# A new load order on two queues, a bf16 product for u, and half of the stores on GpSimd's queue, in an attention and MoE kernel on one core

## The chip, the cores and the metric

The kernel runs on one core of a Trainium2 chip. The metric is the time of one execution on the device in us; lower is better. A profile is one execution with the hardware profiler; its span, from the first instruction to the last, is some 2 us shorter than the time. A run over 1.5% above the fastest of its kernel is called slow, the others fast. Ratios and profiles are of fast runs unless a sentence says otherwise; medians are of all runs, slow ones too (one of the changed kernel's four in the result, three of a_dummy's six). PE is TensorE, PEld its weight loads, ACT ScalarE, DVE VectorE, POOL GpSimd, SP SyncE; a "q" behind a name is that engine's sequencer, which issues transfers. A transfer has landed when its data are there and its semaphore, a counter that others wait for, says so.

## The reference

Inputs r, k, v, w are 4 x 8 x 768 x 48 (batch, heads, tokens, width) in fp32, u is 8 x 48, w_in 384 x 1024, w_out 1024 x 384. The output is 3072 x 384, fp32.

```python
# attention, for each token t
cur = einsum('bhd,bhe->bhde', u * k[t], v[t])
y[t] = einsum('bhd,bhde->bhe', r[t], state + cur)
state = w[t][..., None] * state + einsum('bhd,bhe->bhde', k[t], v[t])
# x: y as 3072 tokens x 384, then
h = x @ w_in
solu = h * softmax(h)
ln = (solu - mean(solu)) / sqrt(var(solu) + 1e-6) * g_ln
out = ln @ w_out
```

## The kernel before

The 3072 tokens are 24 units of 128 (chunk c of batch b). A unit needs four loads of 192 KB (w, k, r, v). What each engine does, and in which order, is written in one string, ORDER. Each word is a stage, a unit number and, after the point, who does it or which PSUM bank it uses: `LW5.s` loads w of unit 5 from SP's queue, `LV4.a` loads v of unit 4 from ScalarE's. Every engine keeps to the written order, so **a transfer that cannot be issued holds up everything that is written behind it on the same engine**.

```python
ORDER = """
... kr2.d y0.a p3 M1.b0 LK5.a S1.s2 dg2 krk3.s3 vb2.a m1.d krr3 et1 wi0.a S2.s0 wi1.p M2.b1 st1 X0.s1 kr3.a m2.d
Y1.is2 LR4.s wi2.p et2 y1.a M3.b0 xT0.d LV4.a X1.s3 q3 m3.d H0.b1 dv2 gw1.a dg3 gw2.d e0 Y2.is2 LW5.s xT1.d
gw3.p st2 H1.b0 y2.a he0 lw4 gw0.a X2.s1 LR5.s e1 gw7.d cum4.b1 gw4.d hot2.s3 gw6.d gw5.d ex4 he1 vb3.p mn0.s3
LW6.s LV5.a dv3 xT2.a LK6.s kp4 S3.s0 mc0 Y3.is2 LR6.s lw5 ce6.d krk4.s1 ce3.d hq0.a cum5.b0 ce4.d krr4 ce2.d
H2.b1 ce7.d ex5 LW7.s ce1.d ce5.d ce0.d y3.a LK7.s p4 kp5 et3 Oa0.s3 ...            # cut: the other lines
"""
NIO = 7                                   # input buffers of each kind

queue = {"s": sp, "a": act}

def load_w(i, x):                         # LW; LK, LR, LV are alike
    queue[x].dma_start(out=w_t[i % NIO][:, :, :D], in_=rows_of(w, i))

def load_w_in(j, x):                      # LI: a third of w_in, 512 KB
    queue[x].dma_start(out=win_f[:, j, :], in_=moe_w_in[j * 128:(j + 1) * 128, :])

def load_w_out(j, x):                     # LO: a half of w_out, 768 KB
    part = slice(j * KF // 2, (j + 1) * KF // 2)
    queue[x].dma_start(out=wout_f[:, part, :],
                 in_=moe_w_out.rearrange("(ko ki) d -> ki ko d", ki=128)[:, part, :])

def spread_u(i, x):                       # us
    ps["u"] = bank([C, DM], F32, x, "u_ps")
    pe.matmul(ps["u"], lhsT=ones_row, rhs=u_row, start=True, stop=True)

def cast_w_in(j, x): ...                  # wi: a third of w_in to bf16
def gain(f, x): ...                       # gw: an eighth of w_out times g_ln, to bf16
def column_mean(i, x): ...                # mn, mc: mean of w_out's columns, on TensorE
def centre(f, x):                         # ce: an eighth of w_out less that mean
    (dve if x == "d" else pool).tensor_add(out=w2[:, f, :DM], in0=w2[:, f, :DM], in1=mean_sb)

def warm_up(i, x): ...                    # hot: i products that nobody reads

def store(i, x):                          # out
    c, b = units[i]
    sp.dma_start(out=out[b * S + c * C:b * S + (c + 1) * C, :], in_=o_t[i % NWK])
# ... cut: a unit's stages: lw, cum, ex, kp, krk/krr (transposes), M (scores), Y (attention), S (state),
#     X (x transposed), H (hidden, needs all of w_in), e and he and hq (exp, product, square),
#     Oa/Ob (output product, needs all eighths of w_out centred), sq/qm/lv/o (variance and scale)
```

The softmax here doesn't subtract the row's maximum and nothing guards it: scores larger than these inputs give would overflow.

Of the kernel before, what the change touches and what calls it, by code (L numbers as in the profile page):

```python
# [555 lines left out]
```

## Time and profile before

| | before |
|---|---|
| time, median of 3 runs | 154.34 us (153.63 to 155.8) |
| span of the profiled run, granted clock | 151.6 us, 0.994 |
| busy share PE / DVE / ACT / POOL | 91 / 84 / 78 / 63% |
| first exp of the hidden layer (e0) starts | 24.51 us |
| cumulative sum of unit 5 starts | 31.63 us |
| mean of w_out's columns copied | 31.16 us |
| first output product starts | 33.73 us |
| last output product ends | 147.2 us |

The prediction below shows the lines for the first reading. One row and one group are added here, because the changed kernel answers to them: the clock granted to TensorE in 40 slices (tenths), and VectorE's timeline (start, busy time, engine, line, operation, tiles, count, idle time before it).

```profile
PEclk9999999999999999999999999999999999999997
...
31.19 2.48 DVE L89 TENSOR_TENSOR w<-w,mean_sb 128x384 bf16<-128x384 bf16 x8 [0.35 <-ACT mean_sb L89]
```

The row tells of no throttling up to the end, but its first record is of 13 us. Before that TensorE was slower: one cumulative product takes 0.50 us at 12.81 us and 0.33 from 14 us on. The eight subtractions of the mean, the last thing that the first output product waits for, take 0.31 us each.

### The profile page before, as it was taken

Reading aid. Unit: us, or ns where it says so; the run is one execution under the profiler, and the core shown is the slowest. Engines: PE = TensorE matmul, PEld = TensorE weight load, DVE = VectorE, ACT = ScalarE, POOL = GpSimd, SP = SyncE. Lnnn points to the kernel's source line nnn. Section 1 sums busy time; section 2 is a strip of 40 time slices with the busy share of each in tenths; the row PEclk is TensorE's granted clock in tenths of the full one; section 3 lists DMA queues with packets and bytes.
Section 4 is the critical chain, followed back from the end, with each engine's and each line's share of the span. In section 5 each row is a group of like instructions: output and inputs, shape, how many; then the busy total and the mean of one; then the engine's idle time right before and its main releaser. Section 6 shows DMA issues by size and latency. Waiting matters only on the chain.

```text
span 151.6 us, 5258 instructions
## 1 busy us (share of the span) xinstructions
PE 137.2 (91%) x2156; PEld 106.6 (70%) x2158; DVE 127.9 (84%) x235; ACT 117.9 (78%) x238; POOL 94.9 (63%) x127
## 2 busy tenths in 40 slices
PE   4799787879999997999988999999999999999980
PEld 1145566467788776888777797878887888889650
DVE  5209797999999996999976999999998998688940
ACT  3465766599999997999798688999898997484442
POOL 7484993531879859993849999299847682500000
PEclk9999999999999999999999999999999999999997
DMA  5999999999983999989699999898950111011142
GB/s 110 259 257 334 405 335 255 178 210 188 224 179 121 229 217 193 215 176 241 142 243 208 230 175 232 162 230 193 248 164 6 52 56 52 4 52 56 52 160 104
DMA packets 104825, 27.08 MB, mean 179 GB/s; under 512 B 100313, under 2 KB 104418, under 8 KB 104802
## 3 DMA queue, kind: packets, MB, share of 16 engines
q1 hardware_dynamic: 94256, 24.26, 69.6%
q10 hardware_dynamic: 10546, 2.49, 7.3%
q8 instruction: 17, 0.28, 0.7%
q14 instruction: 6, 0.05, 0.1%
HBM read 22.03 MB, written 4.72 MB: 176 GB/s over the span
## 4 chain that ended last, share of the span: by engine, by line
PE 54%; DMA 12%; SPq 10%; DVE 8%; ACT 6%; POOL 4%; issue 4%; ACTq 0%; POOLq 0%
PE o_ps L89 22%; PE h_ps L89 13%; SPq L89 10%; DMA w_in<-in_w_dram 6%; PE kr_ps L89 4%; PE y_ps L89 4%; DMA kr_in<-in_r_dram 4%; PE s_ps L89 3%; PE cum_ps L89 3%; PE m_ps L89 3%; DMA v_in<-in_v_dram 3%; PE x_ps L89 2%; DVE he L89 1%; POOL m L89 1%; DVE w L89 1%
## 5 line engine op out<-in xcount | busy, mean ns | idle before, releaser
L89 PE MATMUL o_ps<-w,he 128*128 128x385 bf16 x192 | 45.7, 325 | 0.1
L89 PE MATMUL h_ps<-xT,win_sb 128*128 128x128 bf16 x576 | 35.9, 219 | 0.3 <-DVE xT L89 0.3
L89 PEld LDWEIGHTS <-win_sb 128*128 128x128 bf16 x576 | 33.0, 98 | 0.9 <-issue 0.4
L89 PE MATMUL o_ps<-inv_col,e 128*128 128x1 bf16 x192 | 31.7, 165 | 0.0
L89 DVE TENSOR_TENSOR he<-h_ps,e 128x1024 bf16<-128x1024 f32 x24 | 29.1, 1216 | 2.7 <-ACT e L89 2.5
L89 PE MATMUL o_ps<-one_col,hq 128*128 128x1 bf16 x192 | 31.3, 163 | 0.0
L89 ACT ACTIVATE e<-h_ps 128x1024 bf16<-128x1024 f32 x24 | 24.5, 1020 | 4.7 <-PE h_ps L89 4.6
L89 DVE TENSOR_TENSOR kp<-cum_ps,kr_in 128x768 bf16<-128x768 f32 x24 | 22.7, 948 | 5.9 <-ACT cum_ps L89 5.6
L89 PEld LDWEIGHTS <-hq 128*128 128x128 bf16 x192 | 18.5, 96 | 12.8
L89 POOL TENSOR_TENSOR p<-kr_in 128x384 bf16<-128x384 f32 x24 | 24.4, 1018 | 3.7 <-DMA kr_in<-in_r_dram 3.6
L89 POOL TENSOR_TENSOR dv<-vb,dg 128x384 bf16<-128x384 bf16 x24 | 19.8, 830 | 9.6 <-DVE dg L89 7.4
L89 POOL TENSOR_SCALAR_AFFINE_SELECT m<-m 128x1024 bf16<-128x1024 bf16 x15 | 16.8, 1120 | 13.4 <-ACT sq L89 5.8
L89 POOL TENSOR_TENSOR q<-p,u_bc 128x384 bf16<-128x384 bf16 x24 | 21.8, 911 | 1.9 <-ACT u_bc L89 1.7
L89 PEld LDWEIGHTS <-kp 128*128 128x128 bf16 x272 | 17.4, 98 | 6.0 <-DVE kp L89 2.1
L89 ACT ACTIVATE cum_ps<-cum_ps 128x768 f32<-128x768 f32 x24 | 19.2, 802 | 3.0 <-PE cum_ps L89 2.9
L89 PE MATMUL kr_ps<-ident,kp 128*128 128x128 bf16 x192 | 18.0, 222 | 2.3 <-ACT gr L89 0.8
L89 PEld LDWEIGHTS <-he 128*128 128x128 bf16 x192 | 18.4, 96 | 0.9
L89 PEld LDWEIGHTS <-e 128*128 128x128 bf16 x192 | 18.4, 96 | 0.5 <-issue 0.2
L89 ACT ACTIVATE lw<-w_in 128x384 bf16<-128x384 f32 x24 | 12.4, 523 | 4.1 <-DMA w_in<-in_w_dram 4.1
L89 ACT CAST m<-m_ps 128x1024 bf16<-128x1024 f32 x15 | 15.0, 1013 | 0.7 <-PE m_ps L89 0.6
L89 DVE TENSOR_TENSOR m<-m_ps,keep 128x1024 bf16<-128x1024 f32 x9 | 10.9, 1215 | 4.2 <-PE m_ps L89 4.2
L89 ACT ACTIVATE hq<-he 128x1024 bf16<-128x1024 bf16 x13 | 13.7, 1057 | 0.0
(82 smaller groups left out, 262.5 us busy)
## 6 DMA issues: line engine op xcount, KB each, us to landing
kr_in<-in_r_dram SPq DMA_DIRECT2D x24, 192.0 KB, 4.3
out_dram<-o SPq DMA_DIRECT2D x24, 192.0 KB, 3.2
kr_in<-in_k_dram SPq DMA_DIRECT2D x21, 192.0 KB, 3.5
w_in<-in_w_dram SPq DMA_DIRECT2D x21, 192.0 KB, 4.2
v_in<-in_v_dram SPq DMA_DIRECT2D x20, 192.0 KB, 4.1
...
```

The source lines that it names most:

```text
L89: made = make(*args, **kwargs)
```

## The change

It is meant to get the inputs in earlier by giving ScalarE's queue 17 of the front's loads in place of 12, in a new order, to make u's product one pass, and to free SP of the later stores. Three of the eight subtractions of the mean go from VectorE to GpSimd.

```diff
 ORDER: first line and what matters of the front (all of the string is new)
-LW0.a LK0.s LU0.a LR0.s LW1.a LW2.s hot4.s3 LG0.s LK1.s lw0 LV0.a ...
+LW0.a LW1.s LU0.a LR0.s LK0.a LR2.s hot5.s3 LK1.a LW2.s LR1.a lw0 LG0.a LV0.s ur0 lw1 us0.s0 LW3.a ...
+et0 m1.d LV3.a q2 LI0.s gc0 lw4 LI1.a kp2 cum3.b0 LW5.s Y0.ns3 st0 ex3 cum4.b1 krk2.s1 y0.d vb1.a LO1.s kp3
+X0.s2 LI2.a krr2 dv1 LK5.s ex4 xT0.d krk3.s0 dg2 p3 Y1.ns3 LW6.s S1.s2 kr2.a kp4 p4 LO0.a M2.b0 krr3 et1 m2.d
+vb2.a krk4.s1 q3 kr3.a krr4 dv2 y1.d vb3.a M3.b1 dg3 LV4.a Y2.is0 wi1.p st1 S2.s3 LR5.a kr4.d wi0.a m3.d M4.b0
+wi2.p X1.s2 S3.s1 y2.a et2 LV5.a X2.s0 m4.d dv3 H0.b1 gw1.a xT1.d gw0.d H1.b0 et3 gw3.d e0 LK6.s q4 st2 st3 lw5
 ... cut; the centring: ce4.d ce3.d ce1.d ce0.d ce6.p ce7.d ce2.p ce5.p; the stores: out0 to out11, out12.p to out23.p
-ones_row = consts.tile([1, C], F32)
+ones_row = consts.tile([1, C], BF16)
+u_b = consts.tile([1, DM], BF16)
-queue = {"s": sp, "a": act}
+queue = {"s": sp, "a": act, "p": pool}
+def round_u(i, x):                        # ur
+    dve.tensor_copy(out=u_b, in_=u_row)
-    pe.matmul(ps["u"], lhsT=ones_row, rhs=u_row, start=True, stop=True)
+    pe.matmul(ps["u"], lhsT=ones_row, rhs=u_b, start=True, stop=True)
-    sp.dma_start(out=out[...], in_=o_t[i % NWK])
+    queue[x or "s"].dma_start(out=out[...], in_=o_t[i % NWK])
```

More of the change, by code (lines that the diff above doesn't have):

```diff
@@ L21 @@
 ORDER = """
-LW0.a LK0.s LU0.a LR0.s LW1.a LW2.s hot4.s3 LG0.s LK1.s lw0 LV0.a cum0.b0 LR1.s us0.s0 ex0 hot2.s3 uc0 lw1 LV1.s
-p0 kp0 LW3.a LK2.a LR2.s krk0.s3 q0 krr0 cum1.b1 kr0.a hot2.s2 LV2.s LK3.a M0.b0 LR3.s p1 gs0.s1 ex1 m0.d
-hot3.s3 LI1.s lw2 q1 dg0 cum2.b0 lw3 hot2.s3 kp1 vb0.p LI0.a S0.s2 dv0 vb1.a dg1 hot1.s3 ex2 Y0.is0 et0 LV3.a
-cum3.b1 LI2.s p2 kp2 krk1.s3 gc0 LO0.s ex3 st0 LW4.s krk2.s1 q2 krr1 LO1.s krr2 kp3 kr1.a hot3.s2 dv1 LK4.s
-kr2.d y0.a p3 M1.b0 LK5.a S1.s2 dg2 krk3.s3 vb2.a m1.d krr3 et1 wi0.a S2.s0 wi1.p M2.b1 st1 X0.s1 kr3.a m2.d
@@ L27 @@
-Y1.is2 LR4.s wi2.p et2 y1.a M3.b0 xT0.d LV4.a X1.s3 q3 m3.d H0.b1 dv2 gw1.a dg3 gw2.d e0 Y2.is2 LW5.s xT1.d
-gw3.p st2 H1.b0 y2.a he0 lw4 gw0.a X2.s1 LR5.s e1 gw7.d cum4.b1 gw4.d hot2.s3 gw6.d gw5.d ex4 he1 vb3.p mn0.s3
-LW6.s LV5.a dv3 xT2.a LK6.s kp4 S3.s0 mc0 Y3.is2 LR6.s lw5 ce6.d krk4.s1 ce3.d hq0.a cum5.b0 ce4.d krr4 ce2.d
-H2.b1 ce7.d ex5 LW7.s ce1.d ce5.d ce0.d y3.a LK7.s p4 kp5 et3 Oa0.s3 lw6 e2 LR7.s kr4.d p5 krk5.s2 cum6.b0 st3
-hq1.a Ob0 vb4.p he2 LW8.s q4 krr5 ex6 S4.s1 LK8.s kr5.d sq0 M4.b1 lw7 Oa1.s0 kp6 et4 m4.a LR8.s X3.s2 qm0 st4
@@ L32 @@
-vb5.p M5.b0 xT3.a cum7.b1 dg4 sel4 lv0 krk6.s1 LV6.s Ob1 m5.d ex7 LW9.s dv4 lw8 S5.s2 kp7 o0.a krr6 LK9.s p6
-cum8.b0 sq1 et5 Y4.ns3 kr6.d ex8 H3.b1 q5 LV7.s y4.d hq2.a kp8 q6 LR9.s krk7.s1 e3 X4.s3 st5 LW10.s vb6.p M6.b0
-krr7 xT4.d Oa2.s2 dg5 m6.a LK10.s qm1 kr7.d dv5 krk8.s3 lv1 Ob2 he3 out0 sel6 o1.a lw9 M7.b0 out1 dg6 S6.s1 sq2
-m7.a LV8.s hq3.d krr8 cum9.b1 LR10.s Y5.ns0 vb7.p qm2 kr8.d lv2 H4.b0 p7 LW11.s et6 y5.d ex9 st6 p8 lw10 kp9
-LV9.s X5.s3 S7.s0 e4 Oa3.s1 q7 o2.d vb8.a he4 out2 cum10.b1 dv6 xT5.a krk9.s2 et7 LK11.s ex10 Y6.ns3 q8 krr9 st7
@@ L37 @@
-LV10.s H5.b0 hq4.a kp10 sel7 LR11.s kr9.a y6.d M8.b1 dg7 LW12.s S8.s0 lw11 m8.d Ob3 dv7 et8 e5 LV11.s vb9.p
-krk10.s3 st8 X6.s2 LK12.s p9 M9.b1 he5 xT6.a Y7.ns0 sq3 m9.a krr10 LR12.s S9.s2 dg8 cum11.b0 et9 LW13.s y7.d
-H6.b1 lw12 dv8 ex11 kr10.d LK13.s p10 qm3 lv3 kp11 Oa4.s0 LR13.s e6 q9 st9 X7.s3 cum12.b0 LW14.s xT7.a Ob4 he6
-p11 ex12 LV12.s krk11.s2 sel9 sq4 Y8.ns3 o3.a kp12 H7.b1 hq5.a out3 vb10.p qm4 y8.d q10 LK14.s lv4 dg9 M10.b0 e7
-Oa5.s1 LR14.s m10.d vb11.p q11 o4.a krr11 LW15.s X8.s3 lw13 dg10 Ob5 p12 xT8.a out4 he7 kr11.a S10.s0 dv9 S11.s3
@@ L42 @@
-LV13.s dg11 sq5 hq6.a Y9.ns2 vb12.p qm5 cum13.b0 y9.d dv10 LK15.s H8.b1 et10 ex13 st10 LR15.s et11 lw14 kp13
-Oa6.s2 LW16.s e8 hq7.d krk12.s0 lw15 M11.b0 p13 st11 LK16.s Ob6 lv5 he8 o5.a q12 krr12 m11.a Y10.ns3 out5 kr12.d
-krk13.s1 cum14.b1 LR16.s y10.d sq6 krr13 sel11 ex14 cum15.b0 LW17.s kr13.d Oa7.s0 ex15 qm6 LV14.s kp14 p14
-Y11.ns3 lw16 X9.s1 Ob7 kp15 lv6 dv11 LK17.s vb13.a xT9.d p15 o6.a M12.b1 y11.d M13.b0 m12.a X10.s1 out6 m13.d
-krk14.s2 q13 S12.s3 LR17.s hq8.a krr14 H9.b1 dg12 LV15.s vb14.p xT10.d sq7 q14 et12 qm7 st12 LW18.s lv7 krk15.s1
@@ L47 @@
-dg13 e9 X11.s3 sel12 H10.b0 o7.d kr14.a out7 he9 dv12 LK18.s Y12.ns0 xT11.a p16 krr15 LR18.s Oa8.s2 e10 y12.d
-kr15.d q15 LV16.s cum16.b1 he10 S13.s0 ex16 dv13 Ob8 LV17.s et13 kp16 q16 X12.s3 LW19.s Y13.ns1 sq8 xT12.a st13
-M14.b0 vb15.p M15.b1 LK19.s m14.a y13.d krk16.s3 S14.s0 hq9.d krr16 LR19.s m15.a S15.s1 p17 qm8 kr16.d H11.b0
-LW20.s et14 dg14 lv8 sel14 st14 et15 LK20.s dg15 H12.b1 e11 vb16.p o8.d sel15 st15 out8 lw17 Oa9.s3 he11 LV18.s
-e12 vb17.p dv14 S16.s0 LV19.s hq10.a he12 Ob9 dv15 LR20.s et16 cum17.b0 st16 q17 Y14.ns2 LV20.s ex17 X13.s1
@@ L52 @@
-y14.d M16.b1 sq9 Oa10.s0 lw18 kp17 LW21.s m16.a Y15.ns2 qm9 xT13.d LK21.s cum18.b0 hq11.d lv9 krk17.s1 lw19
-H13.b1 LR21.s o9.d p18 vb18.a dg16 ex18 LV21.s y15.d dv16 krr17 e13 Ob10 kp18 LW22.s sel16 X14.s3 hq12.a kr17.d
-S17.s2 LK22.s cum19.b0 q18 he13 Oa11.s1 xT14.a LR22.s ex19 p19 X15.s3 lw20 M17.b1 out9 xT15.d Ob11 sq10 kp19
-vb20.p m17.a LW23.s q19 Y16.ns3 qm10 dg17 et17 vb19.a cum20.b0 p20 LV22.s y16.d lv10 H14.b1 dg18 sq11 ex20 sel17
-LK23.s st17 lw21 o10.d LR23.s Oa12.s3 e14 kp20 dv17 krk18.s2 Ob12 out10 hq13.a p21 qm11 he14 krk19.s0 LV23.s
@@ L57 @@
-lv11 krr18 q20 cum21.b0 sq12 o11.d krr19 ex21 H15.b1 p22 qm12 kr18.d out11 lv12 kr19.d vb21.p Oa13.s1 dv18 kp21
-e15 X16.s2 o12.d Y17.ns0 xT16.a M18.b0 hq14.a y17.d out12 krk20.s3 Ob13 he15 lw22 X17.s0 m18.a krk21.s2 xT17.d
-krr20 cum22.b1 dg19 krr21 sq13 sel18 ex22 qm13 S18.s0 dg20 H16.b0 kr20.d hq15.a q21 kr21.d lv13 kp22 Oa14.s3
-dv19 e16 dv20 M19.b1 et18 Y18.ns2 he16 m19.a Ob14 lw23 sel19 y18.d M20.b1 sq14 M21.b0 o13.d Oa15.s2 m21.a st18
-out13 m20.d krk22.s1 X18.s0 cum23.b0 xT18.a krr22 Ob15 ex23 hq16.d vb22.p dg21 kr22.a Y19.ns0 q22 kp23 H17.b1
@@ L62 @@
-vb23.a dv21 qm14 sq15 y19.d lv14 Y20.ns1 e17 p23 o14.d H18.b0 dg22 out14 sel21 qm15 y20.d lv15 krk23.s0 he17 e18
-Oa16.s3 dv22 krr23 o15.a he18 q23 Ob16 kr23.a out15 X19.s1 M22.b1 xT19.d M23.b0 hq17.d X20.s2 S19.s0 xT20.a
-hq18.d Oa17.s1 m22.a dg23 Y21.ns2 et19 m23.a sel22 st19 H19.b1 sq16 sel23 qm16 y21.d lv16 Oa18.s0 e19 dv23
-X21.s2 Ob17 he19 H20.b0 sq17 o16.d xT21.d out16 Y22.ns3 qm17 e20 Y23.ns2 y22.d Ob18 y23.d hq19.a he20 H21.b1
-lv17 o17.d X22.s3 Oa19.s2 e21 out17 xT22.d hq20.d X23.s1 sq18 H22.b0 he21 xT23.d Ob19 qm18 hq21.d e22 H23.b1
@@ L67 @@
-sq19 lv18 qm19 he22 Oa20.s3 e23 o18.d hq22.d Oa21.s1 out18 lv19 he23 Ob20 o19.d Ob21 sq20 hq23.d out19 Oa22.s0
-sq21 qm20 qm21 lv20 Oa23.s2 lv21 o20.d o21.d out20 Ob22 out21 Ob23 sq22 qm22 lv22 sq23 qm23 o22.d lv23 out22
-o23.a out23
+LW0.a LW1.s LU0.a LR0.s LK0.a LR2.s hot5.s3 LK1.a LW2.s LR1.a lw0 LG0.a LV0.s ur0 lw1 us0.s0 LW3.a cum0.b0 LK2.s
+cum1.b1 hot2.s3 ex0 p0 uc0 kp0 LW4.a q0 ex1 krk0.s3 p1 krr0 LK3.a LV1.s kp1 hot4.s2 kr0.a q1 dg0 LR3.s lw2 M0.b0
+krk1.s1 m0.d LK4.s gs0.s2 vb0.p krr1 lw3 S0.s0 dv0 cum2.b1 LV2.a kr1.d LR4.s hot1.s3 p2 ex2 dg1 M1.b0 hot4.s3
@@ new lines @@
+et0 m1.d LV3.a q2 LI0.s gc0 lw4 LI1.a kp2 cum3.b0 LW5.s Y0.ns3 st0 ex3 cum4.b1 krk2.s1 y0.d vb1.a LO1.s kp3
+X0.s2 LI2.a krr2 dv1 LK5.s ex4 xT0.d krk3.s0 dg2 p3 Y1.ns3 LW6.s S1.s2 kr2.a kp4 p4 LO0.a M2.b0 krr3 et1 m2.d
+vb2.a krk4.s1 q3 kr3.a krr4 dv2 y1.d vb3.a M3.b1 dg3 LV4.a Y2.is0 wi1.p st1 S2.s3 LR5.a kr4.d wi0.a m3.d M4.b0
+wi2.p X1.s2 S3.s1 y2.a et2 LV5.a X2.s0 m4.d dv3 H0.b1 gw1.a xT1.d gw0.d H1.b0 et3 gw3.d e0 LK6.s q4 st2 st3 lw5
+gw2.p he0 e1 LR6.s gw7.a gw5.d cum5.b1 gw4.d Y3.is2 gw6.d ex5 dg4 vb4.p mn0.s3 he1 LW7.s xT2.a dv4 y3.a S4.s1
@@ new lines @@
+kp5 mc0 Y4.is0 LV6.s lw6 X3.s2 ce4.d hq0.a krk5.s3 ce3.d cum6.b0 ce1.d LK7.s H2.b1 ce0.d et4 xT3.d ex6 vb5.p st4
+ce6.p y4.a LR7.s kp6 krr5 e2 S5.s2 X4.s1 ce7.d LW8.s krk6.s0 et5 ce2.p H3.b0 lw7 he2 hq1.a LK8.s ce5.p xT4.d
+cum7.b1 kr5.d e3 vb6.p LR8.s krr6 Oa0.s1 st5 p5 ex7 kr6.d LW9.s S6.s3 p6 hq2.a Ob0 kp7 LK9.s q5 Oa1.s2 sq0 lw8
+qm0 he3 LR9.s et6 p7 lv0 cum8.b1 krk7.s0 ex8 Ob1 LW10.s dg5 q6 st6 o0.a krr7 LV7.s p8 kp8 sq1 M5.b0 Oa2.s3 m5.a
+kr7.d dv5 LV8.s krk8.s1 lw9 qm1 dg6 M6.b1 sel5 M7.b0 LK10.s m6.a krr8 m7.d Ob2 lv1 LR10.s sel6 cum9.b1 hq3.a
@@ new lines @@
+kr8.d Y5.ns0 H4.b0 out0 o1.d vb7.p ex9 y5.d dv6 LW11.s sq2 lw10 qm2 Y6.ns1 kp9 vb8.p lv2 Oa3.s2 q7 LK11.s e4
+y6.d X5.s0 p9 o2.d cum10.b1 LR11.s S7.s1 he4 ex10 krk9.s3 LV9.s q8 Ob3 xT5.a kp10 hq4.a q9 M8.b0 out1 krr9 dg7
+X6.s0 p10 H5.b1 et7 sq3 m8.a kr9.d out2 qm3 dv7 LV10.s dg8 xT6.a Y7.ns3 st7 LW12.s lv3 dv8 krk10.s0 e5 y7.d
+H6.b0 dg9 LK12.s vb9.p o3.a sel8 he5 lw11 krr10 LR12.s X7.s1 S8.s3 e6 q10 xT7.d Oa4.s2 LW13.s kr10.a he6 p11
+cum11.b1 Y8.ns1 LK13.s ex11 S9.s0 y8.d lw12 M9.b0 kp11 LV11.s Ob4 et8 m9.a st8 cum12.b1 LR13.s sq4 hq5.d
@@ new lines @@
+krk11.s1 ex12 H7.b0 dg10 vb10.p LW14.s et9 dv9 lw13 qm4 kp12 lv4 krr11 LK14.s sel9 Oa5.s3 e7 st9 kr11.d out3
+cum13.b1 o4.a vb11.p Ob5 he7 ex13 dv10 out4 X8.s0 S10.s1 p12 LV12.s kp13 xT8.a Y9.ns2 LR14.s et10 lw14 M10.b0
+q11 y9.d M11.b1 sq5 m10.a krk12.s0 st10 LW15.s S11.s2 qm5 m11.d krr12 lv5 X9.s1 sel10 H8.b0 LK15.s et11 o5.a
+xT9.d hq6.a p13 dg11 LR15.s cum14.b1 kr12.d krk13.s3 q12 ex14 Oa6.s1 st11 out5 e8 q13 kp14 krr13 Ob6 LW16.s lw15
+p14 he8 krk14.s0 sq6 Y10.ns2 LK16.s hq7.a cum15.b1 dv11 kr13.d krr14 H9.b0 ex15 LR16.s vb12.p y10.d LV13.s p15
@@ new lines @@
+hq8.a kr14.d Oa7.s3 qm6 kp15 q14 e9 LW17.s Y11.ns2 dg12 krk15.s0 lv6 y11.d M12.b1 dv12 o6.a krr15 he9 Ob7 m12.a
+out6 X10.s1 LK17.s X11.s2 sq7 hq9.a xT10.d sel12 M13.b1 LR17.s qm7 M14.b0 xT11.d S12.s1 m13.d lw16 Oa8.s2 vb13.p
+LV14.s kr15.a q15 m14.d H10.b1 LW18.s et12 lw17 lv7 st12 LK18.s Ob8 o7.d e10 dg13 LR18.s M15.b0 sq8 dv13 S13.s0
+qm8 m15.a he10 Y12.ns1 out7 Y13.ns3 lv8 sel15 cum16.b0 dg14 LW19.s H11.b1 y12.d ex16 y13.d p16 et13 LV15.s lw18
+kp16 Oa9.s1 e11 vb14.p LV16.s st13 p17 cum17.b0 o8.a dg15 LK19.s X12.s3 X13.s0 Ob9 he11 ex17 dv14 xT12.a S14.s2
@@ new lines @@
+out8 xT13.a kp17 krk16.s3 sq9 lw19 cum18.b1 Y14.ns0 LR19.s vb15.p ex18 krr16 hq10.d H12.b0 et14 kr16.a LW20.s
+dv15 st14 qm9 kp18 lv9 Oa10.s2 q16 LK20.s e12 LV17.s y14.d S15.s3 p18 dg16 M16.b1 et15 he12 o9.a Ob10 q17 LR20.s
+m16.a X14.s0 st15 krk17.s1 out9 sq10 cum19.b0 lw20 qm10 hq11.d krr17 ex19 krk18.s3 H13.b1 xT14.d LW21.s kr17.d
+vb16.a lv10 kp19 dv16 LV18.s krr18 e13 Oa11.s0 sel16 LK21.s cum20.b0 he13 LV19.s Ob11 p19 ex20 krk19.s1 hq12.a
+q18 kp20 H14.b1 o10.a dg17 vb18.p vb17.a kr18.d krr19 out10 p20 sq11 M17.b0 e14 LR21.s qm11 kr19.d Y15.ns2
@@ new lines @@
+Oa12.s3 LW22.s y15.d q19 lv11 m17.a LV20.s o11.d krk20.s1 S16.s2 dv17 he14 Ob12 lw21 sel17 out11 hq13.a krr20
+M18.b0 kr20.d LK22.s vb19.p M19.b1 et16 sq12 m18.a Oa13.s0 q20 st16 LV21.s dg18 m19.a X15.s1 sel18 cum21.b0 qm12
+xT15.d Y16.ns2 LR22.s ex21 Ob13 y16.d dv18 LW23.s lv12 Y17.ns1 hq14.d lw22 X16.s2 H15.b1 o12.a y17.d sel19 sq13
+xT16.a dg19 out12.p qm13 kp21 Y18.ns3 e15 Oa14.s1 y18.d lv13 X17.s2 he15 krk21.s3 H16.b0 hq15.d Ob14 vb20.p
+xT17.d e16 o13.d p21 krr21 out13.p cum22.b1 sq14 qm14 he16 Oa15.s2 vb21.p LK23.s ex22 q21 LV22.s S17.s0 kr21.a
@@ new lines @@
+kp22 LR23.s Ob15 dv19 et17 lv14 st17 p22 M20.b0 sq15 o14.d M21.b1 m20.a Y19.ns3 hq16.d out14.p S18.s0 lw23
+X18.s1 LV23.s qm15 q22 y19.d H17.b0 et18 lv15 xT18.d m21.a sel20 o15.d Oa16.s3 dg20 out15.p e17 dv20 krk22.s1
+X19.s2 cum23.b1 he17 p23 Ob16 ex23 krr22 dg21 sq16 H18.b0 kr22.a qm16 kp23 dv21 lv16 xT19.d Y20.ns1 dg22 o16.a
+krk23.s2 y20.d H19.b1 e18 out16.p hq17.d sel21 he18 krr23 e19 Oa17.s3 S19.s1 kr23.a he19 Ob17 hq18.a st18 X20.s2
+M22.b0 M23.b1 sq17 xT20.a qm17 Oa18.s0 hq19.d m22.a q23 Y21.ns2 m23.a Ob18 y21.d vb22.p lv17 dv22 X21.s2 H20.b0
@@ L70 @@
+o17.a sel22 et19 xT21.a out17.p st19 H21.b1 e20 vb23.p sel23 sq18 qm18 Y22.ns3 dg23 e21 Oa19.s2 y22.d dv23 he20
+lv18 X22.s1 Y23.ns3 o18.a Ob19 xT22.d out18.p hq20.a y23.d H22.b0 he21 sq19 X23.s0 Oa20.s1 e22 xT23.d hq21.d
+H23.b1 qm19 he22 lv19 Ob20 o19.d e23 hq22.d out19.p Oa21.s3 sq20 he23 Oa22.s0 hq23.d Ob21 qm20 lv20 Oa23.s2 sq21
+qm21 o20.d lv21 Ob22 out20.p Ob23 sq22 qm22 o21.d lv22 sq23 out21.p qm23 o22.d lv23 out22.p o23.a out23.p
 """
@@ L509, in store @@
         c, b = units[i]
-        sp.dma_start(out=out[b * S + c * C:b * S + (c + 1) * C, :], in_=o_t[i % NWK])
+        queue[x or "s"].dma_start(out=out[b * S + c * C:b * S + (c + 1) * C, :], in_=o_t[i % NWK])
     stages = dict(
         LW=load_w, LK=load_k, LR=load_r, LV=load_v, LU=load_u, LG=load_g, LI=load_w_in, LO=load_w_out,
-        us=spread_u, uc=copy_u, gs=turn_g, gc=copy_g, wi=cast_w_in, gw=gain, mn=column_mean, mc=copy_mean,
+        ur=round_u, us=spread_u, uc=copy_u, gs=turn_g, gc=copy_g, wi=cast_w_in, gw=gain, mn=column_mean, mc=copy_mean,
         ce=centre, hot=warm_up,
```

## The prediction

> **What bounds the kernel now.** I read the busy slices first, then the chain that ended last, then ScalarE's timeline where that chain is odd, then the busy time by stretches. The slices (40 of 3.79 us):
>
> ```profile
> PE   4799787879999997999988999999999999999980
> ACT  3465766599999997999798688999898997484442
> DMA  5999999999983999989699999898950111011142
> GB/s 110 259 257 334 405 335 255 178 210 188 224 179 121 229 217 193 215 176 241 142 243 208 230 175 232 162 230 193 248 164 6 52 56 52 4 52 56 52 160 104
> ```
>
> The DMA engines are full from the start to 112 us, when the last inputs land; after that TensorE alone works. TensorE is nearly full from 32 us on. The chain of waits says what each stretch costs:
>
> ```profile
> 26.07 3.79 DMA w_in<-in_w_dram
> 29.88 0.37 ACTq L89
> ...
> 30.67 0.49 ACT mean_sb L89
> ...
> 31.72 1.97 DVE w L89 x7
> 33.73 0.99 PE o_ps L89 x12
> ...
> 140.38 5.98 PE o_ps L89 x84
> ```
>
> From 33.73 us, the first product with the output weights, to TensorE's end at 146.4 us the chain is mostly TensorE. I priced each stage from this chain: two cumulative sums 0.33 us, eight transposes 0.47, scores 0.33, state 0.46, attention 0.43, x transposed 0.18, hidden 1.34, output 1.66: 5.2 us for a unit, 124 us for 24. At 33.73 us the written order has 109.2 us of this left, and TensorE ends 112.7 us later: only 3.5 us are lost in that part. The other loss, 33.73 - (124 - 109.2) = 19 us, lies in front. Behind TensorE come 5.2 us of tail (sums, scale, last store). So the time is: the lost front, plus fixed TensorE work, plus a few lost us, plus the tail. The view of busy time by stretches agrees (columns: us, busy PE, PEld, DVE, ACT, POOL, clock, DMA share, GB/s):
>
> ```profile
> 31.60:60.00 28.40, 27.77 (x465) 22.56 (x465) 26.99 (x49) 26.38 (x54) 18.84 (x23) 1.00 0.93 193
> 60.00:95.00 35.00, 33.09 (x576) 27.30 (x576) 32.46 (x53) 30.79 (x62) 29.04 (x35) 1.00 0.98 208
> 95.00:146.40 51.40, 51.40 (x874) 42.55 (x873) 46.78 (x84) 40.45 (x86) 25.27 (x29) 1.00 0.41 102
> ```
>
> What holds up the front is in ScalarE's timeline:
>
> ```profile
> 21.02 0.48 ACT L89 CAST y<-y_ps 128x384 bf16<-128x384 f32 x1 [0.27 <-PE y_ps L89]
> 23.51 0.37 ACTq L89 DMA_DIRECT2D v_in<-in_v_dram  x1
> 23.99 0.62 ACT L89 ACTIVATE w<-wout_f,gr 128x384 bf16<-128x384 f32 x1 [2.48 <-DMA v_in<-in_v_dram]
> 24.51 1.00 ACT L89 ACTIVATE e<-h_ps 128x1024 bf16<-128x1024 f32 x1
> ...
> 29.88 0.37 ACTq L89 DMA_DIRECT2D v_in<-in_v_dram  x1
> 30.30 0.48 ACT L89 COPY xT<-x_ps 128x384 bf16<-128x384 bf16 x1 [1.87 <-DMA w_in<-in_w_dram]
> ```
>
> ScalarE does not compute for 2.48 and 1.87 us because a load that it issues itself waits. In the compiled program every SP or ACT transfer takes one of eight semaphores and waits until that semaphore's previous transfer has landed. v of unit 4 waits for v of unit 3 (landed 23.49), v of unit 5 for w of unit 6 (landed 29.86). The exp, copies and w logs behind stand still meanwhile.
>
> **What the Trainium skill says.** "DMA: Bandwidth & Descriptors", Anatomy of one DMA: semaphore waits of a transfer happen on the issuing sequencer before dispatch. The two stalls are just that. The same page, Issuing engines are not separate DMA queues: all issuers share the same 16 DMA engines, so a second issuer saves only issue time. The trace partly disagrees: small loads run at 262 GB/s from 2 to 14 us with two queues in use, and at 203 GB/s from 26 to 112 us with one. One 196.6 KB load is then 0.75 or 0.97 us. The same page, SWDGE vs HWDGE vs iDMA: GpSimd's transfers have their descriptors made by its own cores; its table of latencies gives first bytes after about 1 us, against 0.6. "SBUF — State Buffer", SBUF: two separate sides: VectorE operations in a two-port mode can keep GpSimd from writing them. No run here shows either yet.
>
> **The change, part by part.**
>
> u's product. fp32 takes two passes, 1.64 us busy at 5.6 us; bf16 takes one, perhaps 0.5. A tiny VectorE cast is added. TensorE waits next for kp (VectorE, done 7.5 us), so it gains 0 to 0.5 us.
>
> Stores. Twelve leave SP. SP waited 25.3 us in all for VectorE's o, but only 0.9 us of it before 112 us, and 1.4 us for ScalarE's: removing it can fill the thin slices near 46 and 72 us (shares 3 and 6), not move TensorE after 95 us. GpSimd gets 12 issues of about 1 us each (estimate from the skill's latency) where it is 49% busy (25.27 of 51.4 us). The last store is in the tail: 1.84 us from issue to landing now; I add 0.5 to 1 us.
>
> Other moves: VectorE loses five scaled outputs and three of the eight subtractions (-3.0, -0.9 us), gains three xT copies; ScalarE gains about 1 us in total. Small.
>
> The new load order is the large part. ACT issues 17 transfers in front instead of 12. The built program says what the late ones wait for: a third of w_in waits for another third, the next third for half of w_out, the other half of w_out for **w of unit 6**, r of unit 5 for **v of unit 6**, v of unit 5 for **r of unit 7**. SP runs ahead, so those targets are late in the stream. When do they land? In the trace, 15 unit loads had landed by 14.16 us, 0.75 us each from 2.9 us, and 25 plus all five weight pieces (3.15 MB) by 29.86 us. 29.86 - 2.9 - 25 x 0.75 leaves 8.2 us for the weights. With that:
> - w of unit 6 lands after 22 unit loads and most weights: 24 to 25.5 us. ScalarE waits there, with the copy of k/r 3 behind.
> - v of unit 6: 26 to 27 loads and all but some of w_out: 29 to 31 us. The cast of the last third of w_in stands behind it, so hidden of unit 0 (21.84 us now) starts near 32.
> - r of unit 7: 28 to 30 loads and all weights, 32.1 to 33.6 us, later if one queue runs dry. Take 33.3.
>
> Behind the last one ScalarE has, in this order: gain 0.6, state exp 0.2, e0 1.0 (starts near 34.3; now 24.51), w log of unit 5 0.5. So the cumulative sum of unit 5 starts near 36 us; it starts at 31.63 now. TensorE's work left at that point is alike: 111.1 us before, 111.9 after. Hence TensorE cannot end before 36 + 111.9 = 148, against 146.4 measured. Behind it come e1 1.0, gain 0.6, decay 0.8, two copies 1.0, column mean 0.5, then three subtractions on GpSimd (2.5): first output product near 44 to 45 us with 104.2 us left, so 148.2 to 149.2. Add 2.5 us lost later (3.5 now; inputs will be further ahead): TensorE ends near 151. Plus tail 5.2 and GpSimd's extra 0.7: span 156.9. The three times have a median 2.7 us over the traced span, the profiled run 1.7; 156.9 + 2.7 is 159.6; I choose to take 1.4 off, because in such a sum of waits some overlap better than counted, and predict **158.2 us**.
>
> **Rivals.**
> 1. The order works as meant: fewer warm-up products (16 for 19), 5 us less TensorE work left at the first output product, weights not crowding the inputs. If the first output product came at 33.7 us as now, the gain would be 109.2 - 104.2 = 5 us: 149 us. Against: five more loads lie ahead of ScalarE's release, 3.8 to 4.9 us.
> 2. Even: ScalarE's stalls overlap with waits for data that TensorE has anyway, and later losses shrink from 3.5 to near 0 because the units start with full input buffers and SP is free of stores. 153 to 157 us.
> 3. GpSimd becomes the bound: at 72 to 82 us the chain already runs through its p, q, dv and mask. Issues in order behind o (which waits for sums and scale) hold back bonus and mask of later units. It had 26 us of slack after 95 us, so I expect 0 to 2 us, more if VectorE locks it out.
> 4. TensorE's clock: it will idle over 3 us in pieces between 26 and 36 us, and "TensorE: Matmul & The Clock Gate", HAM oscillation, says that such gaps halve the clock. The trace before only shows eight transposes taking 1.01 us at 8.4 us and twelve 0.83 us at 16.1. Up to 2 us more.
>
> **Range and chances.** A faster result by 2% needs under 151.3 us; that contradicts the 148 us floor unless r of unit 7 lands 4 us earlier than counted: 0.06. Slower by 2% is over 157.4 us; centre 158.2, with rivals 2 and 3/4 on either side: 0.58. Within 2%: 0.36. Range 153.2 to 162.8 us.
>
> **What would show it.** Right: ScalarE with idle of several us before issues of w_out, r and v between 18 and 35 us, e0 after 32 us, unit 5's cumulative sum after 34 us, first output product after 41 us; TensorE slices 6 to 9 thinner; slices 12 and 19 of DMA fuller; stores from GpSimd landing later than 1.84 us in the tail. Wrong: e0 before 28 us, or a first output product before 37 us: then landings or waits are not as counted. Loss after 45 us above 4 us would make GpSimd's stores, not the front, the cause.

## The result

| | before | after |
|---|---|---|
| time, median of 4 runs each | 153.99 us | 163.55 us (161.84 to 164.4) |
| span, granted clock | 151.6 us, 0.994 | 161.6 us, 0.937 |
| e0 starts | 24.51 | 36.98 |
| cumulative sum of unit 5 starts | 31.63 | 39.32 |
| mean of w_out's columns copied | 31.16 | 42.77 |
| first output product starts | 33.73 | 50.13 |
| last output product ends | 147.2 | 156.02 |

The ratio is 1.0614, 95% interval 1.0474 to 1.0754: **slower by 6%**. A ratio is always the mean time of one kernel's fast runs over that of the other's fast runs of the same rounds, so it isn't quite the ratio of the medians. 163.55 us is just above the predicted range (153.2 to 162.8).

I read the profile after in the same order. The slices of the busy share, of 4.04 us each and counted from 0, and the clock:

```profile
PE   5497444569969999999999999998999999999960
...
PEclk9999975556999999999999999999999999999996
DMA  5999999999910195996988897989998211011113
```

From slice 4 to slice 8 (16 to 36 us) TensorE is half idle, and in slices 5 to 9 its clock is down. From slice 12 on it is as full as before. The DMA engines are nearly idle in slices 11 to 13. ScalarE's timeline of the front shows what happens there (columns as above; what ended the idle time stands behind the arrow):

```profile
25.23 0.46 ACTq L88 DMA_DIRECT2D wout_f<-in_moe_w_out_dram  x1
25.73 0.18 ACT L88 ACTIVATE et<-s_ps 128x8 f32<-128x8 f32 x1 [2.60 <-PE kr_ps L88]
...
31.93 0.43 ACTq L88 DMA_DIRECT2D kr_in<-in_r_dram  x1
32.40 1.04 ACT L88 CAST win_sb<-win_f 128x1024 bf16<-128x1024 f32 x1 [4.77 <-DMA v_in<-in_v_dram]
...
34.31 0.41 ACTq L88 DMA_DIRECT2D v_in<-in_v_dram  x1
34.82 0.62 ACT L88 ACTIVATE w<-wout_f,gr 128x384 bf16<-128x384 f32 x1 [0.92 <-DMA kr_in<-in_r_dram]
...
36.98 1.02 ACT L88 ACTIVATE e<-h_ps 128x1024 bf16<-128x1024 f32 x1 [1.48 <-PE h_ps L88]
```

Each pair is a transfer that ScalarE issues (ACTq) and the computation behind it. The 4.77 us are the plainest: the cast of w_in stands behind the issue of r of unit 5, and that issue came 0.02 us after v of unit 6 had landed (31.91 us). The chain that ended last goes through the same places (start, duration, what):

```profile
25.22 6.69 DMA v_in<-in_v_dram
...
31.93 0.43 ACTq L88
...
32.40 1.04 ACT win_sb L88
...
34.38 2.57 PE h_ps L88 x24
...
42.80 1.50 DVE w L88 x3
...
50.29 0.81 PE o_ps L88 x10
```

The span can be taken apart with the prediction's own sum. Of its 124 us of TensorE work, 109.2 us (before) and 104.2 us (after) are left at the first output product. "Lost in front" is the start of that product less the work done by then:

| us | before | predicted | after |
|---|---|---|---|
| work done before the first output product | 14.8 | 19.8 | 19.8 |
| lost in front | 18.9 | 24.7 | 30.3 |
| work left | 109.2 | 104.2 | 104.2 |
| lost later | 4.3 | 2.5 | 1.7 |
| tail behind TensorE | 4.4 | 5.9 | 5.6 |
| span | 151.6 | 157 | 161.6 |

(The prediction took TensorE's end before as 146.4 us, from the chain; the records of the products end at 147.2 us. That shifts 0.8 us from the tail to "lost later".) The whole loss is in front: 11.4 us more there, 2.6 us won later, 1.2 us more in the tail.

### The profile page after: what moved, and what is told of

Its sections match the earlier page's. It is cut to its first block, busy times and chain, and to the rows that moved or that the text cites. A ratio compares the mean times of both kernels' runs of the same rounds, so it can differ in the third digit from the quotient of the medians.

```text
span 161.6 us, 5258 instructions
## 1 busy us (share of the span) xinstructions
PE 138.6 (86%) x2152; PEld 109.3 (68%) x2153; DVE 128.8 (80%) x231; ACT 118.6 (73%) x238; POOL 106.3 (66%) x144
## 4 chain that ended last, share of the span: by engine, by line
PE 41%; SPq 19%; ACT 11%; DMA 10%; issue 8%; DVE 6%; POOL 2%; POOLq 0%; ACTq 0%
SPq L88 19%; PE o_ps L88 14%; PE h_ps L88 12%; DMA w_in<-in_w_dram 6%; DMA v_in<-in_v_dram 4%; PE kr_ps L88 3%; ACT e L88 3%; PE y_ps L88 3%; PE s_ps L88 3%; DVE w L88 3%; PE m_ps L88 3%; PE cum_ps L88 2%; DVE he L88 2%; ACT hq L88 2%; ACT cum_ps L88 2%
## 5 line engine op out<-in xcount | busy, mean ns | idle before, releaser
L88 PE MATMUL h_ps<-xT,win_sb 128*128 128x128 bf16 x576 | 38.1, 226 | 0.5 <-DVE he L88 0.5
L88 PEld LDWEIGHTS <-win_sb 128*128 128x128 bf16 x576 | 35.5, 102 | 1.0 <-issue 0.6
L88 POOL TENSOR_TENSOR p<-kr_in 128x384 bf16<-128x384 f32 x24 | 23.9, 998 | 1.5 <-DMA kr_in<-in_k_dram 1.5
L88 PEld LDWEIGHTS <-kp 128*128 128x128 bf16 x272 | 18.1, 101 | 6.5 <-DVE kp L88 3.8
L88 POOL TENSOR_SCALAR_AFFINE_SELECT m<-m 128x1024 bf16<-128x1024 bf16 x15 | 17.3, 1156 | 6.6 <-ACT m L88 5.1
L88 PE MATMUL kr_ps<-ident,kp 128*128 128x128 bf16 x192 | 19.0, 228 | 2.5 <-DVE kp L88 2.4
L88 POOL DMA_DIRECT2D out_dram<-o x12 | 7.0, 580 | 14.4 <-DVE o L88 11.2
L88 PEld LDWEIGHTS <-kr 64*128 64x128 bf16 (+1 forms) x272 | 10.5, 98 | 7.9 <-ACT kr L88 4.6
```

Source lines behind the costliest of these rows:

```text
L88: made = make(*args, **kwargs)
```

## The experiments

The theory: the loss is ScalarE standing still behind transfers that it issues, above all r and v of unit 5. Rivals: the bytes or the second queue; GpSimd's stores; the halved clock; the subtractions given to GpSimd. The experiments came in four sets, each on one chip together with the kernel before. All results were correct. A row with - and + is an edit of words of ORDER.

### Two loads back to SP, then six

```diff
 a_two_sp:  -LR5.a +LR5.s   -LV5.a +LV5.s
 a_six_sp:  the same, and  -LI1.a +LI1.s   -LI2.a +LI2.s   -LO0.a +LO0.s   -LV4.a +LV4.s
```

> The changed kernel, but the loads of r and v of unit 5 are issued by SP instead of ScalarE. Theory (waits): ScalarE's idle of 4.8 and 0.9 us at 27 to 34 us goes, the third cast of w_in starts near 28 us, hidden of unit 0 near 30 (34.2 in the changed kernel); 157.5 to 160.5 us. Rival (stores on GpSimd): nothing moves, 163 to 164. Rival (clock alone): the clock stays low until TensorE is busy again, gain under 1.5 us.

> The changed kernel, but all six late front loads of ScalarE (two thirds of w_in, half of w_out, v of unit 4, r and v of unit 5) are issued by SP at the same places of the order. Theory (waits): none of ScalarE's idle stretches over 1.5 us between 17 and 35 us is left, exp of unit 0 starts at 26 to 30 us (36.98), first output product at 38 to 43 us (50.3); 153 to 157.5 us. Rival (stores): 162 to 164. If transfers issued by one queue are too slow in front, first output product later than 45 us and over 159 us.

Measured: two loads give 157.47 us, ratio 1.0249 (1.0166 to 1.0332); six give 154.62 us, 1.0091 (0.9991 to 1.0191). Against the 1.0614 of the result, which is of other rounds, changing only who issues them, and so where they stand in SP's order, took back some 3.6 points, then another 1.6. The hidden layer's first two products, 34.17 us in the changed kernel, started at 30.80 and 25.12 us. With six loads moved, ScalarE never waited to issue in that stretch, but it did wait for the data of the last of them (its timeline):

```profile
29.30 0.62 ACT L88 ACTIVATE w<-wout_f,gr 128x384 bf16<-128x384 f32 x1 [5.65 <-DMA wout_f<-in_moe_w_out_dram]
```

w_out's second half stood behind many unit loads in SP's order. So one wait had been hiding another: the place of w_out's second half in the order was late as well.

### Is it the wait, or the bytes and the queue?

a_two_sp also changes which queue carries two loads of 192 KB. This run keeps those on SP, and gives ScalarE two useless loads of u, 1.5 KB each, at the old places. In the built program the two wait for the landing of r and v of unit 6.

```diff
 a_dummy:  -LR5.a +LR5.s DU0.a     -LV5.a +LV5.s DU1.a
+spare = [consts.tile([1, DM], F32, name=f"spare{j}") for j in range(2)]
+def load_spare(i, x):                     # DU
+    queue[x].dma_start(out=spare[i], in_=u.rearrange("(o h) d -> o (h d)", o=1))
 a_two_again, after_again: a_two_sp and the changed kernel once more, on this chip
```

> The run with r and v of unit 5 issued by SP, plus two useless 1.5 KB loads on ScalarE at the old places. By the built program they wait for r and v of unit 6 to land. Theory (the wait itself): ScalarE stands still again from about 28 to 32 us, first output product near 47 to 50 us (44.7 without the useless loads), 160 to 163 us. Rival (the place of the two real loads in the queues made the difference): 157 to 158.5 us as without them.

> The kernel of a_two_sp again, as the measure for a_dummy on the same chip: ratio to the kernel before 1.02 to 1.03.

> The changed kernel itself, as the measure for the others on this chip: ratio 1.055 to 1.068.

| on one chip | median us | ratio to before (95%) |
|---|---|---|
| after_again | 162.53 | 1.0595 (1.0542 to 1.0649) |
| a_two_again | 156.99 | 1.025 (1.0201 to 1.03) |
| a_dummy | 163.35 | 1.0579 (1.0502 to 1.0656) |

**3 KB at the old places bring the whole loss back.** It is the wait on ScalarE's sequencer, not the bytes and not the queue. (Two more loads also shift the semaphores of all later ones, SP's too. SP was not held back by that: it issued v of unit 6 at 27.98 us, in a_two_again at 28.80.) ScalarE's timeline in a_dummy:

```profile
31.61 0.26 ACTq L88 DMA_DIRECT2D spare<-in_u_dram  x1
31.91 1.04 ACT L88 CAST win_sb<-win_f 128x1024 bf16<-128x1024 f32 x1 [4.24 <-DMA v_in<-in_v_dram]
```

The same cast in a_two_again, where nothing is issued before it:

```profile
28.31 1.05 ACT L88 CAST win_sb<-win_f 128x1024 bf16<-128x1024 f32 x1
```

It starts 3.6 us earlier and without a wait. (The profiled run of a_dummy was its fastest, 161.04 us, and that of a_two_again its slowest, 158.34; their spans, 159.2 and 156.6 us, thus differ by less than the medians.)

### The kernel before has two such stalls too

```diff
 b_two_sp (of before):  -LV4.a +LV4.s   -LV5.a +LV5.s
```

> The kernel before, but v of units 4 and 5 are issued by SP instead of ScalarE. Theory (waits of ScalarE's own loads cost time in both kernels): the two idle stretches of 2.48 and 1.87 us at 21 to 30 us go, first output product 1.5 to 4 us earlier than 33.7; 150 to 152.5 us against 154. Rival: with 4.4 us of ScalarE idle gone TensorE finds the next wait (inputs or weights not there), 153.5 to 155 us.

Measured: 153.52 us, ratio 1.0063 (1.0003 to 1.0122); no gain. ScalarE's two stalls (2.48 and 1.87 us) were gone and the mean was copied at 29.25 instead of 31.16 us, but the first output product came at 34.01 us, before at 33.73. VectorE's timeline says why:

```profile
29.94 4.01 DVE L89 TENSOR_TENSOR w<-w,mean_sb 128x384 bf16<-128x384 bf16 x8
```

The same eight subtractions took 4.01 us in place of 2.48: 1.9 us earlier, they fell beside GpSimd's p, cast and q (29.53 to 32.7 us), which in the kernel before were over by 31.6 us. A stall that is removed is worth only what the next engine can use.

### The stores

```diff
 a_stores_sp:               -out12.p ... out23.p   +out12 ... out23
 b_stores_pool (of before): -out12 ... out23       +out12.p ... out23.p, and the queue "p"
```

> The changed kernel with all 24 stores issued by SP, as before. Theory (waits in front): 162.5 to 165 us, the front as in the changed kernel, tail shorter by 0.3 to 0.7 us. Rival (stores on GpSimd cost the time): 156 to 160 us.

> The kernel before, with the stores of units 12 to 23 issued by GpSimd in the changed kernel's way. From the all-SP run of the changed kernel (162.1 against 163.55) the stores should cost 0.5 to 2 us: 154.5 to 156 us. Rival (GpSimd's stores hold back bonus and mask): over 156.5. Rival (SP freed of stores helps): under 153.5.

Measured: a_stores_sp 162.1 us, 1.0563 (1.0494 to 1.0633), which isn't resolved from the changed kernel's 1.0614. b_stores_pool 154.24 us, 1.0111 (1.0061 to 1.0161): the stores cost the kernel before 1.1%. The part of the page of the changed kernel that lists GpSimd's issues as work (busy, mean ns), and the one that gives the time to landing:

```profile
L88 POOL DMA_DIRECT2D out_dram<-o x12 | 7.0, 580 | 14.4 <-DVE o L88 11.2
...
out_dram<-o POOLq DMA_DIRECT2D x12, 192.0 KB, 2.1
```

A store occupies GpSimd for 0.58 us and lands 2.1 us after its issue in the median. In the tail, where nothing else moves, GpSimd's last store took 2.13 us. SP's last but one in the kernel before, and its last in a_stores_sp, took 1.84 (the landing of the last one before isn't told). So moving the stores accounts for about 1% of the 6% (0.6 to 1.6 by b_stores_pool's interval).

### The clock

The hidden layer's first two products took 5.17 us at half clock, against 2.84 us for the same ones in a_two_sp (3.79 in a_two_again, where the full clock came back while they ran). To measure this by itself, products that nobody reads keep TensorE busy while it waits.

```diff
 a_warm:                  -LV5.a X2.s0  +LV5.a hot8.s0 X2.s0
 a_warm2, a_warm2_again:  -LV5.a X2.s0  +LV5.a hot7.b1 X2.s0
```

> The changed kernel with eight more warm-up products of zeros while TensorE waits for y of unit 2 (30.5 to 33.9 us). If the halved clock in front is a part of the loss: hidden of units 0 and 1 take 1.35 us each instead of 2.6, 161 to 162.3 us. If the clock does not matter (TensorE waits for ScalarE anyway): 163 to 164. Theory (waits) alone holds either way; the clock can be worth 2.5 us at most.

> The changed kernel with seven warm-up products ahead of x of unit 2, this time into a bank that is free by then (the first try wrote the bank that the wait was for, so the products ran after the wait). If the halved clock is a part of the loss: hidden of units 0 and 1 take 3.2 us together (5.2), 161 to 162.3 us. If not: 163 to 164.

> The changed kernel with seven warm-up products in the idle stretch, again beside the changed kernel: if the halved clock costs what hidden of units 0 and 1 showed (5.17 against 2.84 us), 2 to 2.8 us below after_again. If it was the chip: equal.

a_warm went wrong: 165.4 us, 1.0762 (1.0701 to 1.0824). I had given the eight products the bank that X2 waits for, so they ran behind the wait (34.74 to 38.3 us) and not in it. a_warm2 uses a bank that is free there. It gave 160.9 us, 1.0542 (1.0483 to 1.0601); on the chip of the last set 160.87 us, 1.0484 (1.0427 to 1.054), where the changed kernel gave 1.0595. TensorE's timeline of after_again:

```profile
34.48 5.22 PE L88 MATMUL h_ps<-xT,win_sb 128*128 128x128 bf16 x48
```

and of a_warm2_again:

```profile
31.16 2.34 PE L88 MATMUL warm_ps<-warm 128*128 128x512 bf16 x5 [0.22 <-issue]
...
34.54 2.84 PE L88 MATMUL h_ps<-xT,win_sb 128*128 128x128 bf16 x48
```

The 48 products start at the same time, and take 5.22 or 2.84 us. The whole execution gained 1.1% of the time before, 1.7 us; the first output product came 2.07 us earlier (48.41 for 50.48). That is the price of the halved clock at these products. The long wait alone did not halve it: the clock fell at 22 us, before that wait began, and in a_six_sp, without any issue of ScalarE's in the way, it stood at 0.50 from 24 to 30 us. In a_best and a_best_ce (below) it isn't halved in front.

### The subtractions

In the changed kernel three of the eight are GpSimd's and those on VectorE take 0.77 to 0.98 us. Are the three what delays the first output product?

```diff
 a_ce_d:                -ce6.p ce2.p ce5.p   +ce6.d ce2.d ce5.d
 b_ce_pool (of before): -ce6.d ce2.d ce5.d   +ce6.p ce2.p ce5.p
```

> The changed kernel with all eight subtractions of the column mean on VectorE, as before (three of them ran on GpSimd). In the changed kernel VectorE's subtractions took 0.98 us each beside GpSimd's, against 0.31 before. Theory (the two engines block each other): eight take 2.5 to 3.2 us, column mean to first output product 5.5 to 6.5 us instead of 7.36; 161.5 to 162.8 us. Rival (other VectorE work sets that stretch): 163 to 164 us.

> The kernel before with the three subtractions on GpSimd that the change put there. Theory (blocking): VectorE's five take 0.8 to 1.0 us each as long as GpSimd's three run (0.94 each), first output product 0.3 to 1.5 us later than 33.73; 154 to 155.5 us. Rival (GpSimd only takes work off VectorE): 0.9 us earlier, 152 to 153 us.

a_ce_d: 164.53 us, 1.0662 (1.059 to 1.0735), and the first output product at 51.92 us. This theory fell. b_ce_pool is inconclusive: only one of its six runs was fast (152.71 us), and its profile is a slow one. VectorE's timeline of a_ce_d has this line:

```profile
42.27 4.27 DVE L88 TENSOR_TENSOR w<-w,mean_sb 128x384 bf16<-128x384 bf16 x4
```

and that of a_best_ce (below), which has the same eight on VectorE at another moment, this one:

```profile
34.10 1.15 DVE L88 TENSOR_TENSOR w<-w,mean_sb 128x384 bf16<-128x384 bf16 x4
```

Four subtractions take 4.27 us while GpSimd runs p and q (42.21 to 47.3 us), and 1.15 us while it is idle (33.6 to 35.88 us). Taking the three away from GpSimd only let its next work begin beside VectorE's.

### All that was learnt, together

```diff
 a_best:     a_six_sp, and all stores on SP, and  -LO1.s  +LO1.s LI2.s LO0.s  (from their later places)
 a_best_ce:  a_best with  -ce6.p ce2.p ce5.p  +ce6.d ce2.d ce5.d
```

> The changed kernel with the six late loads and all stores on SP and, further, the last third of w_in and the second half of w_out directly behind the first half. In the run with six loads on SP ScalarE still waited 5.65 us for that half of w_out (gain at 29.3 us). Theory: gain of unit 1's row starts before 26 us, first output product at 37 to 41 us (42.4), 150 to 154 us. If inputs behind the weights then come too late, it stays at 153.5 to 156.

> The version of the changed kernel that ran at 152.08 us (six late loads and stores on SP, weights together), with all eight subtractions on VectorE. Theory (blocking): first output product 0.8 to 1.8 us earlier than 40.7, 150.5 to 151.8 us, a little faster than the kernel before. Rival: 152 us.

Measured: a_best 152.08 us beside 153.06 before, ratio 0.9969 (0.9925 to 1.0013). a_best_ce, on another chip, 152.57 us beside 154.95, ratio 0.9881 (0.9825 to 0.9937): within 2%, but **the one version whose interval lies below the kernel before**, and so well below the changed one (1.0595 to 1.0614). Whether the last step helped isn't shown: the two ran on different chips, and by their profiles a_best is the shorter (150.8 us, a_best_ce 151.4). In both, TensorE keeps its clock (0.997 and 1.0), and e0 starts at 27.54 and 27.63 us. So the new order without its waits is as good as the old one or slightly better, not 5 us better: e0 is still 3 us later than before, with more loads in front of it in the order.

## Why the prediction was wrong

Direction, the waits and their places were right; the size was not (158.2 us, measured 163.55), because the stretch from the wait to the first output product was summed too short. By its steps:

**The bound.** Front, fixed work, small later loss, tail. That the balance closes proves nothing, since both losses are what is left over. What tests it is TensorE's own idle time behind the first output product: 2.5 us before (113.47 us, 111.01 busy) and 0.7 after (105.89, 105.23 busy). This held. One slip: by the prediction's own prices the written order adds up to 123.0 us, not 124 (the last four units need no state). So 13.8 and 18.8 us are done in front, "lost in front" is 1.0 larger in every column, and the 111.9 left at unit 5's cumulative sum is 111.0; the differences stay.

**The waits.** All three were found where the built program puts them. v of unit 6 was to land at 29 to 31 us and landed at 31.91; r of unit 7 at 33.3 and landed at 34.28; w of unit 6 at 24 to 25.5 and landed at 25.21. What the Trainium skill's page "DMA: Bandwidth & Descriptors" says in Anatomy of one DMA (the wait is on the issuing sequencer) is what the trace shows: 4.77 us idle, which ended with the landing, 0.02 us of delay and 0.43 us for the issue. a_dummy shows it by itself. Without the last two waits, 3.45 of the 5.95% are gone on one chip.

**The step that failed** is this sentence and the one behind it: "state exp 0.2, e0 1.0 (starts near 34.3 ...)", "So the cumulative sum of unit 5 starts near 36 us", and "then three subtractions on GpSimd (2.5): first output product near 44 to 45 us". It came at 50.13 us, 5.6 us later than the 44.5 between. Three terms of the sum were too small:

1. *The landing*, by 1.0 us: 34.28 for 33.3. Most of it is a miscount: 24 unit loads, not 25, had landed by 29.86 us (the next, k of unit 6, landed at 31.12), so the weights cost 9.0 us, not 8.2, which puts this landing at 34.1.
2. *TensorE's clock*, by 1.7 us of the time (a_warm2_again) or 2.0 us in the trace. I had it as rival 4, "up to 2 us more", had read the skill's page for it, and left it out of the sum. With it, the centre would have been near 160. It acts twice: the hidden product of unit 0, three pieces behind the released cast, took 2.57 us for 1.34, so e0 waited 1.48 us for TensorE after ScalarE was free; then that of unit 1 held up the cumulative sum (39.32 for 36).
3. *From the mean to the first output product*, 7.4 us where the sum had 4.6 (44.5 less 36 and the 3.9 of ScalarE's list). Of these 4.6 only the three subtractions' 2.5 are named: the terms as written give 42.4 us, not 44 to 45. What was left out is TensorE's own work. The new order writes more of it, the hidden products of units 2 and 3 among it, in front of the first output product: between the mean and that product TensorE is busy for 5.57 of 7.36 us, before for 2.18 of 2.57. It is the same work that rival 1 counted as 5 us less left behind. The other 1.75 us are three waits for VectorE (TensorE's timeline):

```profile
46.20 0.17 PE L88 MATMUL s_ps<-off_blocks,halves 128*128 128x8 bf16 x1 [0.91 <-DVE xT L88]
...
47.54 0.40 PE L88 MATMUL kr_ps<-ident,kp 128*128 128x128 bf16 x4 [0.54 <-DVE kp L88]
...
49.57 0.34 PE L88 MATMUL cum_ps<-lw,uti_neg 128*128 128x384 bf16 x1 [0.30 <-DVE he L88]
```

None of them is a wait for a subtraction by name; the last one on VectorE was done at 48.38 us. But VectorE, busy without a pause from 42.80 to 49.5 us, does them in between:

```profile
42.80 3.08 DVE L88 TENSOR_TENSOR w<-w,mean_sb 128x384 bf16<-128x384 bf16 x4
...
46.54 0.94 DVE L88 TENSOR_TENSOR kp<-cum_ps,kr_in 128x768 bf16<-128x768 f32 x1
47.40 0.98 DVE L88 TENSOR_TENSOR w<-w,mean_sb 128x384 bf16<-128x384 bf16 x1
48.30 1.21 DVE L88 TENSOR_TENSOR he<-h_ps,e 128x1024 bf16<-128x1024 f32 x1
```

The five subtractions left to VectorE take 4.06 us, 1.55 at the price of before, because GpSimd works beside them; and kp and he of later units are written between them, and in the lines left out a copy of x (0.34) and a state (0.54). "Loses three of the eight subtractions (-0.9 us)", in the part on other moves, has the wrong sign: VectorE spent 1.6 us more on five than on eight before. The Trainium skill's "SBUF — State Buffer", SBUF: two separate sides, says that GpSimd, when it reads SBUF, and a VectorE operation with two SBUF inputs lock each other out; the trace agrees on VectorE's side (1.07 us a piece beside GpSimd, 0.29 without). The prediction cited the page for writes in a two-port mode only, and put the lock under rival 3, at GpSimd's cost, not at VectorE's.

In order of time: e0 came 2.7 us later than predicted (1.0 for the landing, 1.5 waiting for TensorE), the cumulative sum of unit 5 3.3, the mean 2.9 (42.77 for 39.9), the first output product 5.6. So half of the miss lies before the mean and half behind it. a_warm2_again moved the mean by 2.0 us (41.11 for 43.13) and the first output product by the same, and left the third term as it was.

**"I choose to take 1.4 off"** failed also. Time over span was 1.95 us (163.55 less 161.6); I had used 2.7 less 1.4. That is 0.65 us of the miss, and the reason given for it, that a sum of waits overlaps better than counted, was the wrong way round here: a wait that ended led to a slower stage.

**Lost later** was 1.7 us, predicted 2.5, with inputs further ahead as I said. The DMA gap in slices 11 to 13 is new, and I had not seen it. SP's waits from 36 to 60 us (what was waited for, us in all, times, longest):

```profile
SPq L88 <- ACT sq L88: 12.3, 1, 12.3
```

Stores 0 to 11 are still SP's, and store 0, which had to wait for the late first output, stood ahead of the next loads for 12.3 us. It cost nothing that can be seen: w, k and r of the units up to 10 and v up to 8 had been issued by then, and TensorE was idle for only 0.7 us behind the first output product.

**u's product.** Predicted 0 to 0.5 us. It took 0.47 us for 1.64, but ScalarE copied u at 8.2 us, before at 7.3, because of its place in the order; no run isolates it.

**Stores.** Predicted 12 x 1 us on GpSimd and 0.5 to 1 us in the tail. Measured 12 x 0.58 us, and 1.1% or 1.7 us of the time before (b_stores_pool). The tail behind the last product was 5.31 us in its profile and 4.36 before, so 0.95 of it lies there, 0.3 of that in the longer landing; where the rest comes from is open.

**The rivals.** 1 (149 us) and 2 (153 to 157) fell with e0 at 36.98 us. 3 is small. 4 happened.

**Still open:** u's share; the rest of the stores' 1.1%; how much of VectorE's 1.75 us in the third term is GpSimd's doing (a_best_ce has four of the eight subtractions fast and still 7.7 us from the mean to the first output product, with TensorE busy for 6.0 of them); and b_ce_pool.

## What to carry to other kernels

An engine that computes should not issue a transfer whose semaphore belongs to another one still on its way: look up in the built program what each issue waits for, and put late ones on an engine that does nothing else. (What that gains depends on what comes next: two such loads were worth 3.4 points here and nothing in the kernel before.) Count what is written in front of the product that you wait for, not only what it reads. When a prediction has a stall of TensorE in front of dense products, put those products into the sum at half clock rather than in a list of rivals. And price a stretch by every engine that has work written in it, at the price that its work has beside its neighbour's: the same four subtractions cost 1.15 or 4.27 us here.

## What the Trainium skill lacked or had wrong

- "DMA: Bandwidth & Descriptors", Issuing engines are not separate DMA queues, has a second issuer save the time of initiating, "usually small". It doesn't say what it can cost: two loads of 1.5 KB issued from ScalarE made this kernel 3.2% slower (1.0579 over 1.025), because ScalarE's own work stood behind their waits. It is not shown to be wrong on the rate: the prediction read 262 GB/s with two queues in use against 203 with one, but from 14 to 28 us a_best, with 10 of its 11 loads on SP, moved 323 GB/s, and the changed kernel, with 5 of 15 on ScalarE, 314.
- No page that I read says that SP's and ScalarE's transfers in a built program share eight semaphores, so that one engine's issue waits for the other's landing: v of unit 6, issued by SP, landed at 31.91 us, and ScalarE's load of r of unit 5 went out at 31.93.
- "DMA: Bandwidth & Descriptors", Specifications, gives about 1 us to the first byte for GpSimd and 0.6 for SP and ScalarE, but not the time that the issuing engine spends. The prediction took 1 us for that; the runs show 0.58 us of GpSimd's time for each store, and 2.13 us from issue to landing for its last store, 1.84 for SP's.
- "TensorE: Matmul & The Clock Gate", HAM oscillation, speaks of idle gaps over about 3.4 us (the section after it has micro-idles do it too in another kernel, without a length). Here the clock was halved at 22 us, in the second of two idle gaps, of 1.85 and 2.12 us, with 0.9 us of work between them; none in the 8 us before was as long as 3.4. It was full again at about 39 us, some 5 us after dense products had begun at 34.17. Three stretches of 2 us of the changed kernel show it (us, busy PE, PEld, DVE, ACT, POOL, clock, DMA share, GB/s):

```profile
20.00:22.00 2.00, 0.89 (x21) 0.75 (x21) 0.84 (x3) 0.58 (x1) 2.00 (x3) 0.99 1.22 328
22.00:24.00 2.00, 0.80 (x11) 0.61 (x12) 1.11 (x2) 1.14 (x2) 1.23 (x2) 0.50 1.13 300
...
38.00:40.00 2.00, 2.00 (x26) 1.66 (x24) 1.97 (x4) 1.03 (x3) 0.00 (x0) 0.74 0.91 183
```

- "SBUF — State Buffer", SBUF: two separate sides, has the lock right but gives no time for this operation. Here a subtraction of 128 x 384 in bf16 takes 0.29 us (a_best_ce) without GpSimd and 1.07 us (a_ce_d) beside it.
